# Moving eight vector adds into accumulating DMAs, and a residual update into a DRAM row scatter, in a fused state-space and expert kernel

## The chip, the cores and the metric

The kernel runs on one core of one Trainium2 chip. The metric is device time in microseconds (us) of one execution. Each profile shows one profiled execution; its span is about 2 us shorter than the timed figure of the same run. PE is the matmul engine (PEld its weight load), DVE the vector engine, ACT the scalar engine, POOL the engine that issues the accumulating DMAs, SP the engine that issues most others.

## The reference, cut to what matters

`x` has 2048 rows of 512 columns in bf16. `a` is a long convolution of `x` with a kernel built from 128 complex exponentials per column (done as a transform, spectral products, and an inverse transform) plus a skip term. `b` is `x`, with an expert's output added on the two rows with the largest router score.

```python
g = _sigmoid((x * gate_w).sum(-1, keepdims=True))
a = _A_ref(x, A_re, A_im, ...)          # y = irfft(rfft(x) * rfft(K)) + x * Dskip
# ... in _B_ref: the two rows with the largest r = x @ w_r
g_ = _silu(x_sel @ w_gate); u = x_sel @ w_up
y = (g_ * u) @ w_down                   # times sigmoid(r) of those rows
upd = _scatter_add(zero, flat_idx, y, axis=0)
b = x + upd
return g * a + (1 - g) * b
```

## The kernel before: the parts that matter

The program is a list of operations with their reads and writes. At build time a greedy scheduler orders the operations of each engine by its own cost model, and that order is then fixed. An engine that waits can't do work that comes later in that order, even if it is ready. Nearly all data lies in one on-chip tensor, so the profile names almost every tile `AR`. An operation is told by its source line (a helper's) and its form. Columns are done in two halves of 256 (`h` = 0, 1). The spectral products of each half come in two quarters (`qd`), each with a block 1, then a block 0.

The products of one quarter, all on DVE, with single buffers PA, PBb, PC and YY:

```python
for blk in blks:
    TT(v4(PA), xv(blk), kv(0, 0), MUL, ...)
    if blk == 1:
        TT(v4(PC), xv(0), kv(1, 0), MUL, ...)
        TT(PA, PA, PC, ADD, ...)                 # an add of 128x2048
    TT(v4(PBb), xv(blk), kv(0, 1), MUL, ...)
    if blk == 1:
        TT(v4(PC), xv(0), kv(1, 1), MUL, ...)
        TT(PBb, PBb, PC, ADD, ...)               # another: 8 in all
    TT(v1(YY, 0), v1(PA, 0), v1(PBb, 1), SUB, ...)
    TT(v1(YY, 1), v1(PA, 1), v1(PBb, 0), ADD, ...)
    TT(sd(0), y(0), y(1), ADD, ...); TT(sd(1), y(0), y(1), SUB, ...)
```

The inverse transform of one half (PE), its output gated and added to the residual `U`. For all but the last block, the adding was already a DMA before the change:

```python
# per block, q, t2, parity: 8 matmuls of 256 columns with the matrices G
if h == 0 or blk == 1:
    AC(YA(...), pb(...), ACTF.Copy, ..., scale=g)         # ACT
    g.dma_start(u, YA(...), accum_op=ADD)                  # POOL, 256 KB, rows of 512 B
else:
    STT(u, pb(...), g, u, MUL, ADD, ...)                   # DVE, the last block only
DMA(out, U ...)                                            # the stores
```

`U` was rewritten to `(1 - g) * (x + upd)` by `xupd`: two matmuls and one ACT copy for each of 16 row tiles. The order of the program:

```python
exps1(0); exps2(0)          # 41 exponentials on ACT; a half of exps2 parked in DRAM
routing(); tab1(0); forward(); tab2(0); tab1(1); xupd()
kgen(0); kp load; tab2(1); kspec(0); edges(0); kgen(1)
G load                      # c_inv, 2 MB: the inverse matrices
# kspec(1), products, inverse of both halves, stores
```

Of the kernel before, what the change touches and what calls it, by code (L numbers as in the profile page):

```python
# [9 lines left out]
BF = mybir.dt.bfloat16  # L10
# [44 lines left out]
class Op:  # L55
    __slots__ = ("eng", "fn", "deps", "cost", "tset", "prio", "idx", "pos", "start", "end", "sem", "n", "bl", "vc", "tag", "nbytes", "dma", "name", "alt")


class Prog:
# [4 lines left out]
    def __init__(self):  # L64
        self.bufs, self.ops, self.boost, self.bias = [], [], 0.0, {DVE: 0.4}

    def op(self, eng, fn, rd=(), wr=(), cost=0.2, tset=None, prio=0.0, tag="", n=1, nbytes=0, dma=False):
        o = Op()
        o.alt = None
        if isinstance(eng, tuple):  # L70
            o.alt = dict(zip(eng, zip(fn, cost)))
            eng, fn, cost = eng[0], fn[0], min(cost)
# [34 lines left out]
    def schedule(self):  # L107
# [25 lines left out]
        while left:  # L133
            best = None
            for e0 in ENGS:
                for o in ready[e0]:
                    if o.tset is not None and o.tset != phases[ph[0]]:
                        continue
                    e = e0
                    if o.alt is not None:  # L140
                        e = min(o.alt, key=lambda x: max(free[x], rt[o.idx]) + o.alt[x][1] + self.bias.get(x, 0.0))
                    st = max(free[e], rt[o.idx])
                    key = (st, -o.bl - o.prio)
                    if best is None or key < best[0]:
                        best = (key, o, e)
# [193 lines left out]
def bass_gated_mix__ssm_conv_s4__moe_arch_mod__prompt_kernel(nc, A_u, A_A_re, A_A_im, A_B_re, A_B_im, A_C_re, A_C_im, A_log_dt, A_Dskip,  # L339
# [5 lines left out]
    cb = np.concatenate([eye, np.zeros((128, 384), np.float32), sgn, -sgn], 1)  # L345
# [18 lines left out]
    with ExitStack() as es:  # L364
# [4 lines left out]
        dsem = [es.enter_context(nc.semaphore("d%d" % i)) for i in range(90)]  # L369
# [52 lines left out]

        o_ = [190 * KB]
# [4 lines left out]
        CB = small("cb", 1536, BF); CF = small("cf", 640, F32); AL = small("al", 2048, F32); B16 = small("b16", 2048, F32)  # L428
        WW = small("ww", 2048, BF); SG = small("sg", 256, F32); SGB = small("sgb", 128, BF); RTS = small("rts", 1088, F32)
        OHT = small("oht", 64, BF); ZB = small("zb", 2048, BF); WL = small("wl", 16, BF); XS = small("xs", 16, BF)  # L430
        HB = small("hb", 448, BF); MSB = small("msb", 16, BF); DSK = small("dsk", 1024, BF); OHR = small("ohr", 4096, BF)
# [18 lines left out]
        EB = [B("eb%d" % i, o, NM * 512) for i, o in enumerate((oG, oE))]  # L450
        ST = B("st", oE, NM * 512)
        PK = Buf(P, "park", AR[:, :], "dram", 0, 4, BF)
        park = nc.dram_tensor("park", (128, NM * 256), BF).ap()
# [7 lines left out]
        KC = [B("kc0", oD + 28 * KB, 3 * KB), B("kc1", oE + 11 * KB, 3 * KB)]  # L461
# [4 lines left out]
        PA = B("pa", oI, 4 * KB); PBb = B("pb", oI + 4 * KB, 4 * KB); PC = B("pc", oI + 8 * KB, 4 * KB); YY = B("yy", oI + 12 * KB, 4 * KB); YA = B("ya", oI + 16 * KB, 4 * KB)  # L466
# [30 lines left out]
        DQ([(CB(0, 128, 0, (1, 768)), cb_c[:, :])], [], [CB], 196608, eng=ACT)  # L497
# [14 lines left out]
        for buf, n in ((DSK, D), (OHR, L), (ZB, 2 * D)):  # L512
# [38 lines left out]
        def exps2(ts):  # L551
            for b in (EB[0], ST):
                P.op(POOL, lambda h, b=b: h.memset(b(0, 128, 0, (4 * NM, 64), (1, 4)), 1.0), [], [(b, ("e", 0))], cost=0.4)
            for i, m in enumerate(MAG2):
                if i:
                    AC(two(EB[0], ST, i * 4, 4 * NM), AL(0, 128, 0, (HC, 2), (4, 64), (1, 4)), ACTF.Exp, [AL], [(EB[0], ("e", i)), (ST, ("e", i))], scale=float(m), tset=ts)
# [70 lines left out]
        def routing():  # L627
# [14 lines left out]
            AC(SG(0, 128, 16, (1, 16)), SGB(0, 128, 0, (1, 16)), ACTF.Tanh, [(SGB, "s")], [(SG, "t")], scale=0.5, tset=1)  # L642
            TS(SGB(0, 128, 32, (1, 16)), SG(0, 128, 16, (1, 16)), 0.5, MUL, [(SG, "t")], [(SGB, "g")], s2=0.5, op1=ADD)
            CP(SG(0, 128, 32, (1, 16)), SGB(0, 128, 32, (1, 16)), [(SGB, "g")], [(SG, "g")])
            TS(SGB(0, 128, 48, (1, 16)), SGB(0, 128, 32, (1, 16)), -1.0, MUL, [(SGB, "g")], [(SGB, "o")], s2=1.0, op1=ADD)
            CP(SG(0, 128, 48, (1, 16)), SGB(0, 128, 48, (1, 16)), [(SGB, "o")], [(SG, "o")])
# [22 lines left out]
            AC(R(39), MSB(0, 128, 0, (1, 1)), ACTF.Tanh, [(MSB, 0)], [K("th")], scale=0.5, tset=1)  # L669
# [11 lines left out]
            for hf in range(2):  # L681
                bb = misc(True)
                def tro(h, bb=bb, hf=hf):
                    last = None
                    for t_ in range(8):
                        last = h.transpose(bb(0, 2, t_ * 128, (1, 128)), OHT(0, 128, (hf * 8 + t_) * 2, (1, 2)), IDN(0, (1, 128)))
                    return last
                P.op(PE, tro, [OHT, CB], [bb.buf], cost=0.5)
                EV(OHR(0, 2, hf * 1024, (1, 1024)), bb(0, 2, 0, (1, 1024)), [bb.buf], [(OHR, hf)])
# [14 lines left out]
            AC(hb(2), hb(0), ACTF.Silu, [(HB, 0)], [(HB, 2)], tset=1)  # L704
# [8 lines left out]
            CP(ZB(0, 2, 0, (1, D)), yb(0, 2, 0, (1, D)), [yb.buf], [(ZB, 0)])  # L713
            TS(ZB(0, 2, D, (1, D)), ZB(0, 2, 0, (1, D)), RTS(0, 2, 37, (1, 1)), MUL, [(ZB, 0), K("rs")], [(ZB, 1)])

# [111 lines left out]
        def products(h, qd, blks):  # L827
# [13 lines left out]
            for blk in blks:  # L841
                TT(v4(PA), xv(blk), kv(0, 0), MUL, kx(blk) + kk(0, 0), [PA])
                if blk == 1:
                    TT(v4(PC), xv(0), kv(1, 0), MUL, kx(0) + kk(1, 0), [PC])
                    TT(PA(0, 128, 0, (1, 2048)), PA(0, 128, 0, (1, 2048)), PC(0, 128, 0, (1, 2048)), ADD, [PA, PC], [PA])
                TT(v4(PBb), xv(blk), kv(0, 1), MUL, kx(blk) + kk(0, 1), [PBb])
                if blk == 1:
                    TT(v4(PC), xv(0), kv(1, 1), MUL, kx(0) + kk(1, 1), [PC])
                    TT(PBb(0, 128, 0, (1, 2048)), PBb(0, 128, 0, (1, 2048)), PC(0, 128, 0, (1, 2048)), ADD, [PBb, PC], [PBb])
                TT(v1(YY, 0), v1(PA, 0), v1(PBb, 1), SUB, [PA, PBb], [(YY, 0)])  # L850
                TT(v1(YY, 1), v1(PA, 1), v1(PBb, 0), ADD, [PA, PBb], [(YY, 1)])
                y = lambda pm: YY(0, 128, pm * 512, (1024, 2), (1, 512))
                sd = lambda pm: X(0, 128, h * 8192 + blk * 4096 + pm * 1024 + 2 * qd * 256, (2048, 2), (1, 512))
                kw = lambda pm: [xk(h, blk, part, pm, ft) for part in range(2) for ft in (2 * qd, 2 * qd + 1)]
                TT(sd(0), y(0), y(1), ADD, [YY], kw(0))
                TT(sd(1), y(0), y(1), SUB, [YY], kw(1))
# [3 lines left out]
        def inverse(h):  # L860
            for blk in (1, 0):
                bufs = {}
                for q in range(2):
                    for t2 in range(2):
                        for par in range(2):
# [4 lines left out]
                            def iv(hh, blk=blk, par=par, t2=t2, pb=pb, q=q):  # L870
                                last = None
                                for e in range(2):
                                    for c in range(4):
                                        part, ft = c % 2, 2 * q + c // 2
                                        last = hh.matmul(pb(0, 128, e * 256, (1, 256)), G(0, 128, ((par * 2 + part) * 4 + ft) * 512 + (2 * t2 + e) * 128, (1, 128)),  # L875
                                                         X(0, 128, h * 8192 + blk * 4096 + part * 2048 + (par * 4 + ft) * 256, (1, 256)), start=(q + e + c == 0), stop=(q == 1 and e == 1 and c == 3 and not t2))
# [3 lines left out]
                            P.op(PE, iv, [G] + [xk(h, blk, part, par, ft) for part in range(2) for ft in (2 * q, 2 * q + 1)] + ([KP, CO[h]] if q and t2 else []), [pb.buf], cost=8 * 0.11)  # L880
                            if q == 0:
                                continue
                            if h == 0 or blk == 1:
# [3 lines left out]
                                if par == 1:  # L887
                                    tbs = [blk * 8 + 4 * t2 + k for k in range(4)]
                                    u = U(0, 128, (blk * 8 + 4 * t2) * D + h * HC, (D, 4), (1, HC))
                                    P.op(POOL, lambda g, u=u, t2=t2: g.dma_start(u, YA(0, 128, t2 * 1024, (HC, 4), (1, HC)), accum_op=ADD), [(YA, (p_, t2, e)) for p_ in range(2) for e in range(2)] + [(U, ("x", tb)) for tb in tbs], [(U, ("o", tb, h)) for tb in tbs], cost=1.0, nbytes=262144, dma=True)  # L890
# [9 lines left out]
        def xupd():  # L900
            for tb in range(16):
                pb = fwp[(tb // 2) % 2]
                c0 = (tb % 2) * 512
                def xu(h, tb=tb, pb=pb, c0=c0):
                    h.matmul(pb(0, 128, c0, (1, D)), IDN(0, (1, 128)), U(0, 128, tb * D, (1, D)), start=True, stop=False)  # L905
# [88 lines left out]
```

## Time and profile before

| | before |
|---|---|
| time, median of 4 runs | 188.99 us (187.95 to 191.09) |
| span of the profiled run | 187.5 us |
| DVE busy | 157.1 us |
| first kernel-generation matmul of the second half (PE) | 123.1 us |
| last product on DVE ends | 179.2 us |
| from there to the end | 8.3 us |

The timeline of DVE before, from 120 us on (start, duration, engine, line, operation, count, and in brackets the idle time in front of it):

```profile
119.46 18.89 DVE L399 TENSOR_TENSOR AR<-AR 128x2048 bf16<-128x2048 bf16 x20
139.04 0.42 DVE L399 TENSOR_TENSOR AR<-ps,AR 8x256 bf16<-8x256 f32 x1 [0.69 <-PE ps L823]
139.49 39.68 DVE L399 TENSOR_TENSOR AR<-AR 128x2048 bf16<-128x2048 bf16 x46
180.55 3.71 DVE L406 SCALAR_TENSOR_TENSOR AR<-ps,AR 128x256 bf16<-128x256 f32 x8 [1.38 <-PE ps L875]
```

For sixty microseconds DVE idles 0.7 us, then does the last eight combines as the last inverse matmuls deliver.

### The profile page before, as it was taken

How to read it: one execution, taken by the hardware profiler on the slowest of the kernel's cores; microseconds unless marked ns; L12 is line 12 of the kernel's file. 1: busy time of each engine (PE TensorE's matmuls, PEld its weight loads, DVE VectorE, ACT ScalarE, POOL GpSimd, SP SyncE). 2: the span in 40 equal slices, each digit the busy share in tenths (PEclk: the TensorE clock that was granted, in tenths of full speed). 3: DMA queues.
4: the chain of work that ended last, by engine and by line, in shares of the span. 5: the costliest groups of instructions: out<-in, count | busy, mean ns of one | idle time of the engine just before them, and what ended most of it. 6: DMA issues, size and time to landing. Idle time of an engine off the chain costs nothing.

```text
span 187.5 us, 3219 instructions
## 1 busy us (share of the span) xinstructions
PE 139.4 (74%) x1318; PEld 90.7 (48%) x1318; DVE 157.1 (84%) x232; ACT 126.5 (67%) x210; POOL 12.3 (7%) x17
## 2 busy tenths in 40 slices
PE   0000599675999999999994997379879999375791
PEld 0000236232673444466561366278568888254680
DVE  0629124999999699999689999999989999999962
ACT  3699998999999763389999967637455573402400
POOL 8000000000000000000100000000000050500500
PEclk9999999999996999999999999958999999999998
DMA  5999999994039202200097000000840039591295
GB/s 98 309 300 357 278 258 264 405 378 108 3 91 355 61 0 56 56 3 0 19 416 310 0 3 0 2 0 3 273 180 0 0 40 151 77 154 33 33 146 157
DMA packets 33504, 25.20 MB, mean 134 GB/s; under 512 B 21449, under 2 KB 30802, under 8 KB 33106
## 3 DMA queue, kind: packets, MB, share of 16 engines
q1 hardware_dynamic: 28978, 23.10, 39.9%
q0 software_dynamic: 3168, 1.57, 7.7%
q10 hardware_dynamic: 1344, 0.33, 1.2%
q8 instruction: 10, 0.16, 0.4%
q14 instruction: 4, 0.03, 0.1%
HBM read 17.79 MB, written 2.75 MB: 110 GB/s over the span
## 4 chain that ended last, share of the span: by engine, by line
PE 45%; DVE 32%; ACT 7%; SPq 6%; DMA 4%; issue 3%; DVEq 0%
DVE AR L399 30%; PE ps L732 15%; PE ps L777 6%; PE ps L747 6%; SPq L495 6%; DMA AR<-c_fwd 4%; PE ps L875 4%; PE ps L791 3%; ACT AR L410 3%; ACT AR L414 2%; ACT AR L418 2%; PE ps L750 2%; PE ps L710 2%; PE ps L699 1%; PE ps L813 1%
## 5 line engine op out<-in xcount | busy, mean ns | idle before, releaser
L399 DVE TENSOR_TENSOR AR<-AR 128x1024 bf16<-128x1024 bf16 (+7 forms) x142 | 127.6, 949 | 11.2 <-DMA AR<-in_A_A_re_dram 6.0
L414 ACT ACTIVATE AR<-ps 128x1024 bf16<-128x1024 f32 (+4 forms) x55 | 42.2, 796 | 26.3 <-PE ps L813 11.8
L410 ACT ACTIVATE AR<-AR 128x512 bf16<-128x512 f32 (+5 forms) x73 | 50.4, 755 | 5.6 <-DVE AR L399 2.6
L732 PE MATMUL ps<-AR 128*128 128x512 bf16 x128 | 33.2, 413 | 24.4 <-DMA AR<-c_fwd 20.7
L875 PE MATMUL ps<-AR 128*128 128x256 bf16 x256 | 29.6, 273 | 7.8 <-DVE AR L399 7.8
L732 PEld LDWEIGHTS ps<-AR 128*128 128x128 bf16 x128 | 13.1, 106 | 42.1 <-DMA AR<-c_fwd 20.7
L875 PEld LDWEIGHTS ps<-AR 128*128 128x128 bf16 x256 | 24.7, 98 | 11.6 <-DVE AR L399 8.7
L410 ACT ACTIVATE AR<-ps,AR 128x256 bf16<-128x256 f32 (+1 forms) x40 | 19.8, 575 | 14.4 <-PE ps L875 13.5
L813 PE MATMUL ps<-AR 128*128 128x256 bf16 x160 | 19.2, 273 | 4.7 <-ACT AR L414 4.4
L813 PEld LDWEIGHTS ps<-AR 128*128 128x128 bf16 x160 | 15.0, 98 | 8.6 <-ACT AR L414 6.3
L414 DVE CAST AR<-ps 128x1024 bf16<-128x1024 f32 x6 | 7.3, 1218 | 13.1 <-PE ps L732 9.8
L747 PE MATMUL ps<-AR 128*128 128x512 bf16 x64 | 16.2, 389 | 0.0
L418 ACT ACTIVATE AR<-AR 128x256 int32<-128x256 f32 (+1 forms) x40 | 16.2, 468 | 0.1
L777 PE MATMUL ps<-AR 128*128 128x84 bf16 x256 | 13.7, 221 | 2.8 <-DVE AR L399 2.4
L777 PEld LDWEIGHTS ps<-AR 128*128 128x128 bf16 x256 | 12.7, 110 | 5.2 <-DVE AR L399 2.7
L890 POOL DMA_DIRECT2D AR<-AR x6 | 7.9, 1490 | 76.7 <-ACT AR L410 76.7
L403 DVE TENSOR_SCALAR AR<-AR 128x1024 int32<-128x1024 int32 (+5 forms) x22 | 11.4, 527 | 0.0
L747 PEld LDWEIGHTS ps<-AR 128*128 128x128 bf16 x64 | 5.8, 98 | 5.9 <-issue 0.2
L905 PE MATMUL ps<-AR 128*128 128x512 bf16 x16 | 6.2, 385 | 2.5 <-ACT AR L410 2.5
L791 PE MATMUL ps<-AR 128*32 128x128 bf16 (+1 forms) x96 | 6.4, 383 | 0.7 <-ACT AR L414 0.7
L931 POOL MEMSET AR<- 128x256 bf16 x2 | 0.6, 312 | 88.2 <-PE ps L777 88.2
L906 PE MATMUL ps<-AR 128*128 128x512 bf16 x16 | 6.1, 379 | 0.0
(48 smaller groups left out, 71.2 us busy)
## 6 DMA issues: line engine op xcount, KB each, us to landing
AR<-c_ksp SPq DMA_DIRECT2D x1, 2752.0 KB, 10.2
AR<-in_A_u_dram SPq DMA_DIRECT2D x2, 1024.0 KB, 7.7
AR<-c_fwd SPq DMA_DIRECT2D x1, 2048.0 KB, 8.1
AR<-c_fwdn SPq DMA_DIRECT2D x8, 256.0 KB, 3.8
AR<-c_inv SPq DMA_DIRECT2D x1, 2048.0 KB, 7.6
out_dram<-AR SPq DMA_DIRECT2D x16, 128.0 KB, 2.2
AR<-in_B_w_gate_dram SPq DMA_DIRECT2D x1, 1792.0 KB, 9.9
AR<-in_B_w_up_dram SPq DMA_DIRECT2D x2, 896.0 KB, 10.9
```

Of the source, the lines that this page charges most:

```text
L399: return P.op(DVE, lambda h: h.tensor_tensor(out=o, in0=a, in1=b, op=op), rd, wr, cost=tt_cost(o, a, b), **k)
L403: return P.op(DVE, lambda h: h.tensor_scalar(out=o, in0=a, scalar1=s1, scalar2=None, op0=op0), rd, wr, cost=c, **k)
L410: return P.op(ACT, lambda h: h.activation(out=o, in_=a, func=func, scale=scale, bias=bias), rd, wr, cost=0.185 + nel(o) * 0.833e-3 + (0.09 ...
L414: return P.op((ACT, DVE), (lambda h: h.activation(out=o, in_=a, func=ACTF.Copy), lambda h: h.tensor_copy(o, a)), rd, wr, cost=(0.185 + n * ...
L418: return P.op((ACT, DVE), (lambda h: h.activation(out=o, in_=a, func=ACTF.Copy, scale=c), lambda h: h.tensor_scalar(out=o, in0=a, scalar1= ...
L495: P.op(SP, lambda h: h.dma_start_transpose(PRM(0, 128, i * D, (1, D)), dr(prm[i], 0, (128, D), (1, 128))), [], [(PRM, i)], cost=1.25, nbyt ...
L732: last = h.matmul(o, F(0, 128, ((par * 4 + st) * 2 + part) * 512 + ft * 128, (1, 128)), U(0, 128, (blk * 8 + st * 2 + par) * D, (1, D)), s ...
L747: last = h.matmul(o, ng(0, 128, (st * 2 + part) * 128, (1, 128)), U(0, 128, (blk * 8 + st * 2 + 1) * D, (1, D)), start=False, stop=(st == ...
L777: last = hh.matmul(pb(0, 128, (g - b0) * 84, (1, 84)), TP[h][1 - part](0, 128, g * 128, (1, 128)), TQ[h][1 - part](0, 128, g * 84, (1, 84) ...
L791: last = hh.matmul(pb(32 * g, 32, c4, (256, njg), (4, 64)), lw, KA[h](0, 128, c4 + 4 * (base[0] + g), (16, njg), (84, 64)), start=True, st ...
L813: last = hh.matmul(pb(0, 128, n * 256, (1, 256)), KP(0, 128, u * 2048 + tau * 128, (1, 128)), KC[h](0, 128, jg * 256, (1, 256)), start=(k ...
L875: last = hh.matmul(pb(0, 128, e * 256, (1, 256)), G(0, 128, ((par * 2 + part) * 4 + ft) * 512 + (2 * t2 + e) * 128, (1, 128)), X(0, 128, h ...
```

## The change

The intent: take eight of the 142 vector operations away (the 128x2048 adds) and let DMA do them; take 32 matmuls and 16 ACT copies of the residual rewrite away; take nine exponentials from ACT's first phase.

- The eight adds become accumulating DMAs of 512 KB, issued by POOL. The products get double buffers, and the differences are formed in place.
- The two expert rows are scatter-added to a DRAM copy of the input. That copy is loaded into `U` in place of the input.
- The output becomes `g * (a - b) + b`: 32 added matmuls with a negative identity subtract `b` in the inverse.
- `exps2` moves behind the first sines, without its trip to DRAM.

The diff, cut to its core:

```diff
+        def accum(o, i, rd, wr, nbytes):
+            P.op(POOL, lambda h: h.dma_start(o, i, accum_op=ALU.add), rd, wr, cost=1.4, nbytes=nbytes, dma=True)
...
             for blk in blks:
+                PA, PBb = PAB[qd]
                 TT(v4(PA), xv(blk), kv(0, 0), MUL, kx(blk) + kk(0, 0), [PA])
-                if blk == 1:
-                    TT(v4(PC), xv(0), kv(1, 0), MUL, kx(0) + kk(1, 0), [PC])
-                    TT(PA(...), PA(...), PC(...), ADD, [PA, PC], [PA])
                 TT(v4(PBb), xv(blk), kv(0, 1), MUL, kx(blk) + kk(0, 1), [PBb])
                 if blk == 1:
-                    TT(v4(PC), xv(0), kv(1, 1), MUL, kx(0) + kk(1, 1), [PC])
-                    TT(PBb(...), PBb(...), PC(...), ADD, [PBb, PC], [PBb])
-                TT(v1(YY, 0), v1(PA, 0), v1(PBb, 1), SUB, [PA, PBb], [(YY, 0)])
-                TT(v1(YY, 1), v1(PA, 1), v1(PBb, 0), ADD, [PA, PBb], [(YY, 1)])
+                    for part in range(2):
+                        p, q = (PA, PBb)[part], PCD[h][qd][part]
+                        TT(v4(q), xv(0), kv(1, part), MUL, kx(0) + kk(1, part), [q])
+                        accum(p(0, 128, 0, (1, 2048)), q(0, 128, 0, (1, 2048)), [q], [p], 524288)
+                TT(v1(PA, 0), v1(PA, 0), v1(PBb, 1), SUB, [PBb], [PA])
+                TT(v1(PA, 1), v1(PA, 1), v1(PBb, 0), ADD, [PBb], [PA])
...
+                                    if q:      # in the inverse: minus identity times U
+                                        last = hh.matmul(pb(0, 128, e * 256, (1, HC)), CB(0, 128, 768, (1, 128)), U(...), start=False, ...)
...
-        def xupd(): ...                       # 32 matmuls, 16 ACT copies
-        exps2(0)
-        DMA(park <- ST); ... DMA(EB[1] <- park)
+        exps2(2)
+        DMA([(xp[:, :], dr(A_u, ...))], [], [XP], 2097152, prio=1e5)
...
+            indirect_dma_start(xp[:, :], rows IDX, ZB(0, 2, 0, (1, D)), compute_op=ADD)
+        DMA(U <- xp)                          # 2 MB, after the scatter
-        tab2(0, (1, 1)); tab1(1, (1, 1)); tab2(1, (1, 1))
+        tab2(0, (3, 3)); tab1(1, (3, 3)); tab2(1, (3, 3))   # later phase; tanh, silu too
```

## The prediction

> **What bounds the kernel now.** The page gives DVE 157.1 us busy of 187.5, PE 139.4, ACT 126.5. The table by stretches shows DVE full from about 33 us to 179 us (61 of 64 us up to 97, nearly all after that); the chain of waits is PE and ACT from 33 to 97 us, but alternates with a DVE that is full as well. From 97.6 us it is DVE: second-half table work to 122.3 us, then spectral products to 179.2 us (about 56 us of TENSOR_TENSOR, 2048 columns at 1.15 us spacing, 1024 at about 0.6), then 8.3 us of tail: last inverse matmuls, eight combines of 0.48 us, the store. Before 33 us DVE is half idle; ACT runs 41 exponentials until 28.4 us, 0.52 us apart.
>
> **What the change moves.**
> 1. Eight DVE adds of 128x2048 leave the products: 8 x 1.15 = 9.2 us of a full DVE. Eight accumulating DMAs of 512 KB replace them. The six accumulating DMAs of 256 KB in the trace take 1.3 to 1.75 us to issue and land after 4.2 to 5.4 us; their 512-byte packets take 74 ns against 27 ns for plain stores of that size. Now rows are 4 KB: between 0.28 us (overhead-bound guess) and 0.59 us (linear) a packet, estimated 2.3 to 4.7 us per transfer, one after the other. [...] At the middle, 3.4 us, each half's four accumulations take about 14 us plus 5 us of issue and landing, longer than the multiplications that could hide them, so DVE waits 2 to 4 us per half. Net gain in the products: about 3.5 us (0 if linear, 7 if overhead-bound).
> 2. The residual rewrite goes: 32 PE matmuls (0.22 us each, 7 us), 16 ACT copies (9.8 us), 16 small transposes, one 1.0 us ACT and one 0.67 us DVE copy. They lie beside a full DVE: mostly off the path, about 1 us of gain.
> 3. Subtraction by 32 added PE matmuls of 256 columns: 32 x 0.11 = 3.5 us, of which about 0.9 us in the tail.
> 4. Nine exponentials (4.7 us) move behind the first sines. DVE can start near 28 us instead of 33. But ACT is full until 56 us, and pays two more table loads (1.28 us each), so the second table comes hardly earlier. Gain 1 to 2 us.
> 5. DRAM copy (2 MB), row scatter and 2 MB reload replace the 640 KB park round trip. All are early, off the path; the copy sits ahead of the up-weights, which land near 48 us instead of 42 and are needed at 54.
>
> **Sum.** Minus 2.5 us before 97 us, minus 3.5 us in the products, plus 0.9 us of matmuls and about 0.5 us because the late block's accumulations hold the end: minus 4.6 us. Predicted 184.0 us, range 178.5 to 188.5. Chances: faster 0.60, same 0.31, slower 0.09.
>
> **What the profile would show.** Right: DVE busy near 146 us; DVE waits on the accumulating DMAs of 2 to 4 us in each products stage; 4 KB packets near 0.43 us; ACT with four table loads; 32 more matmuls at the inverse; table stage of the second half starting near 95 us. The first sine would start near 25 us.
>
> **What would make it wrong.** Accumulations at the linear cost, or slowed by the 2 MB inverse-matrix load falling into the first products: no gain at all. Overhead-bound packets: 180 us. The weights or forward matrices held behind the DRAM copy: PE stalls near 50 us. A static order that puts an accumulation behind one that waits.

The 0.59 us is eight times the 74 ns measured for a packet of 512 bytes. The 0.28 us is the author's guess; adding the 47 ns by which that packet is dearer than a plain store to eight times 27 ns would give 0.26 us, an estimate.

## More of the kernel before

From the page of the kernel before: busy time; the rows of the span in 40 slices (tenths; PEclk is the clock that PE was granted); the chain of waits by engine and by line; the costliest group; the load of the inverse matrices.

```profile
PE 139.4 (74%) x1318; PEld 90.7 (48%) x1318; DVE 157.1 (84%) x232; ACT 126.5 (67%) x210; POOL 12.3 (7%) x17
...
DVE  0629124999999699999689999999989999999962
...
PEclk9999999999996999999999999958999999999998
DMA  5999999994039202200097000000840039591295
...
PE 45%; DVE 32%; ACT 7%; SPq 6%; DMA 4%; issue 3%; DVEq 0%
...
L399 DVE TENSOR_TENSOR AR<-AR 128x1024 bf16<-128x1024 bf16 (+7 forms) x142 | 127.6, 949 | 11.2 <-DMA AR<-in_A_A_re_dram 6.0
...
AR<-c_inv SPq DMA_DIRECT2D x1, 2048.0 KB, 7.6
```

DVE is full in nearly every slice from the eighth to the third from the end. The chain gives PE more than DVE, because until about 97 us both are full. From there to the end DVE leads.

## The result, and the profile after

The time rose from a median of 188.99 us to one of 200.97 us (199.51 to 201.10, 4 runs). The ratio is 1.064, with a 95% interval of 1.056 to 1.071. Ratios here are the mean time of one kernel's fast runs over that of the other's fast runs of the same rounds, so they are not quite the ratio of the medians quoted beside them.

| milestone | before | after | added up to here |
|---|---|---|---|
| first kernel-generation matmul, second half | 123.1 | 125.4 | +2.3 |
| last product on DVE ends | 179.2 | 186.7 | +7.5 |
| end of the profiled run | 187.5 | 199.3 | +11.8 |

So in these two profiles 2.3 us are lost before 125 us, 5.2 us in the products, though eight adds went from there, and 4.3 us in the tail (12.6 us in place of 8.3). The first of these is not firm. Nine runs below (e1, e5 to e9, e11, e13 and e16) have the DVE order of the changed kernel up to its first accumulation, and their profiles put the first milestone anywhere from 122.3 to 126.0 us.

The page of the kernel after, with the lines that answer to those of before, and the group of the accumulations:

```profile
PE 141.0 (71%) x1302; PEld 93.4 (47%) x1302; DVE 150.7 (76%) x229; ACT 116.5 (58%) x190; POOL 31.6 (16%) x25
...
DVE  0628129999599999987999999959339997839442
...
PEclk9999999995887999999985998599999999697999
DMA  5999999988039202200599100299920079997195
...
PE 36%; DVE 30%; DMA 23%; SPq 6%; issue 2%; POOL 0%; DVEq 0%
DVE AR L400 24%; DMA AR<-AR 14%; PE ps L731 13%; PE ps L874 6%; SPq L501 6%; PE ps L746 6%; DMA AR<-c_ksp 5%; DMA AR<-c_fwd 4%; PE ps L776 2%; DVE AR L415 2%; PE ps L812 2%; DVE AR L404 2%; PE ps L705 2%; PE ps L749 2%; PE ps L694 1%
...
L400 DVE TENSOR_TENSOR AR<-AR 128x2048 bf16<-128x2048 bf16 (+6 forms) x135 | 118.6, 928 | 25.3 <-DMA AR<-AR 13.6
...
L713 POOL DMA_INDIRECT xp<-AR x1 | 14.5, 14522 | 70.7 <-DVE AR L404 70.7
...
AR<-AR POOLq DMA_DIRECT2D x8, 512.0 KB, 7.7
...
AR<-c_inv SPq DMA_DIRECT2D x1, 2048.0 KB, 11.6
```

DVE did get lighter, by 6.4 us. But its tensor operations now idle 25.3 us in place of 11.2. Over half of that, 13.6 us, is ended by a DMA from `AR` to `AR`, the accumulations. In the chain DMA went from 4% to 23%. The accumulations are 14 of these; 5 are the load of `c_ksp`, where PE waited, but DVE had table work in all that time and did not idle for it. One more line has changed that the change didn't touch: the same 2 MB load of `c_inv` takes 11.6 us in place of 7.6.

The timeline of DVE after, from 120 us on, in the columns of before:

```profile
119.39 11.64 DVE L400 TENSOR_TENSOR AR<-AR 128x2048 bf16<-128x2048 bf16 x13
131.46 1.23 DVE L400 TENSOR_TENSOR AR<-AR 128x2048 bf16<-128x2048 bf16 x1 [0.43 <-DMA AR<-AR]
134.51 6.15 DVE L400 TENSOR_TENSOR AR<-AR 128x2048 bf16<-128x2048 bf16 x7 [1.82 <-DMA AR<-AR]
141.26 0.42 DVE L400 TENSOR_TENSOR AR<-ps,AR 8x256 bf16<-8x256 f32 x1 [0.60 <-PE ps L822]
147.62 18.66 DVE L400 TENSOR_TENSOR AR<-AR 128x1024 bf16<-128x1024 bf16 x22 [5.94 <-DMA AR<-AR]
167.65 5.74 DVE L400 TENSOR_TENSOR AR<-AR 128x1024 bf16<-128x1024 bf16 x7 [1.37 <-DMA AR<-AR]
177.48 9.23 DVE L400 TENSOR_TENSOR AR<-AR 128x1024 bf16<-128x1024 bf16 x13 [4.08 <-DMA AR<-AR]
191.68 0.88 DVE L407 SCALAR_TENSOR_TENSOR AR<-ps,AR 128x256 bf16<-128x256 f32 x2 [4.97 <-PE ps L877]
```

The solid block of before is cut at five places, each time by an accumulation: 8.2 us of waits in the first half, 5.45 us in the second. The prediction had 2 to 4 us for each. Why does an accumulation take so long? Here are the records of the eight in the trace, with what else was on the DMA queues:

| issued, us | landed after, us | what was under way beside it |
|---|---|---|
| 126.8 | 4.6 | nothing |
| 129.1 | 5.4 | the one before, for 2 us |
| 133.0 | 12.1 | the `c_inv` load, issued at 133.65 |
| 136.0 | 11.6 | the same, and the one before |
| 159.7 | 4.7 | nothing at first |
| 160.8 | 6.8 | the one before, then two output accumulations |
| 165.4 | 8.6 | two output accumulations of 256 KB, issued at 161.4 and 162.1 and so ahead of it, and stores |
| 166.6 | 10.9 | the same, and the one before |

The packets themselves were cheap. The records that belong to these DMAs have 4096 bytes each, 1024 of them for eight transfers, with a median of 339 ns, less than the 0.43 us that the prediction assumed. (In the same trace the packets of 512 bytes took a median of 74 ns in the output accumulations and 27 ns in the plain stores.) From 136 to 142 us the records of the 16 DMA engines show about 16 accumulation packets of 4 KB and 16 load packets of 16 KB in each microsecond, one for one: 95 of the one kind and 96 of the other in all. Below, "turns" stands for this sharing as counted here; that each engine alternates strictly between the two was not shown. So each of the 16 engines gets through one accumulation packet in a microsecond there, on average, in place of about three at 131 or at 144 us (49 and 52 packets in that microsecond), when no load is beside it.

In the second half the records show another kind of sharing. There POOL's transfers come in the order of issue. From 167 to 170 us their queue shows only the 512-byte packets of the two output accumulations, 808 of them. The third product accumulation had been issued at 165.4 us, but its packets come after them, from 170 us on.

The tail can be read from the chain of waits after, cut to its end (start, duration, what):

```profile
136.03 11.56 DMA AR<-AR
147.62 17.54 DVE AR L400 x21
...
166.58 10.88 DMA AR<-AR
177.48 3.11 DVE AR L400 x5
180.63 0.61 PE ps L874 x4
...
182.31 0.85 PE ps L874 x4
...
187.06 3.93 PE ps L874 x36
191.10 0.44 PE ps L874 x4
```

The accumulation that landed at 177.5 us was a block 1's. Once it had landed PE still had half of block 1's inverse and all of block 0's to do, and the chain stays on PE from 180.6 us to 195.1 us. From 181.3 to 184.7 us PE ran at half clock: four matmuls took 0.85 us at 182.3 us, 0.44 us at 191.1 us. (The expectations call such a stretch a cold clock.) In this trace the granted clock is at one half in stretches of 3.4 and 6.8 us, two of 3.4 us in the last inverse (from 171.1 and 181.3 us), just after idle times of PE of 4.5 and 4.4 us. In the last inverse of the kernel before, idle times of 3.25 and 3.53 us were followed by no half clock. The second stretch, of 3.4 us at half rate, cost about 1.7 us of the chain, an estimate (half its length).

The front shows the third loss. ACT loads its tables at 24.16, 42.81 and 49.83 us, besides the first, which was there before; the first sine starts at 25.45 us, as predicted. The earlier sines gave DVE table work early, and the routing's small operations fell behind it. The timeline of PE before, in the same columns as DVE's:

```profile
45.90 0.27 PE L655 MATMUL ps<-AR 128*128 128x128 f32 x1
46.01 1.89 PE L732 MATMUL ps<-AR 128*128 128x512 bf16 x8
47.82 1.76 PE L677 MATMUL ps<-AR 128*128 128x2 bf16 x64
```

The timeline of PE after:

```profile
46.30 0.48 PE L659 MATMUL ps<-AR 128*128 128x128 f32 x1 [3.09 <-DVE AR L404]
47.44 3.60 PE L731 MATMUL ps<-AR 128*128 128x512 bf16 x8 [0.66 <-DVE AR L415]
50.83 0.42 PE L659 MATMUL ps<-AR 128*128 128x128 f32 x1
51.04 2.19 PE L731 MATMUL ps<-AR 128*128 128x512 bf16 x8
53.06 1.75 PE L681 MATMUL ps<-AR 128*128 128x2 bf16 x64
```

The gather of the routed rows (64 matmuls of 2 columns) starts at 53.06 us, 5.2 us later than before. This profile is an extreme one: the other runs with late exponentials start it at 50.2 to 52.7 us, those with early ones at 47.8 to 49.5 us. Eight forward matmuls took 3.60 us in place of 1.89, at half clock (granted 0.5 from 44.8 to 51.6 us). The second half's tables, predicted to start near 95 us, started at 101.18 us; before it was 97.57 us.

### The profile page after: what moved, and what is told of

It is laid out like the page before. It is cut to its first block, busy times and chain, and to the rows that moved or that the text cites. A ratio compares the mean times of both kernels' runs of the same rounds, so it can differ in the third digit from the quotient of the medians.

```text
span 199.3 us, 3178 instructions
## 1 busy us (share of the span) xinstructions
PE 141.0 (71%) x1302; PEld 93.4 (47%) x1302; DVE 150.7 (76%) x229; ACT 116.5 (58%) x190; POOL 31.6 (16%) x25
## 4 chain that ended last, share of the span: by engine, by line
PE 36%; DVE 30%; DMA 23%; SPq 6%; issue 2%; POOL 0%; DVEq 0%
DVE AR L400 24%; DMA AR<-AR 14%; PE ps L731 13%; PE ps L874 6%; SPq L501 6%; PE ps L746 6%; DMA AR<-c_ksp 5%; DMA AR<-c_fwd 4%; PE ps L776 2%; DVE AR L415 2%; PE ps L812 2%; DVE AR L404 2%; PE ps L705 2%; PE ps L749 2%; PE ps L694 1%
## 5 line engine op out<-in xcount | busy, mean ns | idle before, releaser
L400 DVE TENSOR_TENSOR AR<-AR 128x2048 bf16<-128x2048 bf16 (+6 forms) x135 | 118.6, 928 | 25.3 <-DMA AR<-AR 13.6
L415 ACT ACTIVATE AR<-ps 128x1024 bf16<-128x1024 f32 (+3 forms) x51 | 39.4, 806 | 36.4 <-PE ps L812 16.6
L731 PE MATMUL ps<-AR 128*128 128x512 bf16 x128 | 34.6, 425 | 22.5 <-DMA AR<-c_fwd 21.9
L874 PE MATMUL ps<-AR 128*128 128x256 bf16 x256 | 35.5, 286 | 10.8 <-DVE AR L400 8.9
L731 PEld LDWEIGHTS ps<-AR 128*128 128x128 bf16 x128 | 13.3, 107 | 40.6 <-DMA AR<-c_fwd 21.9
L425 POOL DMA_DIRECT2D AR<-AR x14 | 14.7, 1178 | 78.0 <-DVE AR L400 61.0
L812 PE MATMUL ps<-AR 128*128 128x256 bf16 x160 | 20.5, 286 | 8.4 <-DMA AR<-c_ksp 5.4
L713 POOL DMA_INDIRECT xp<-AR x1 | 14.5, 14522 | 70.7 <-DVE AR L404 70.7
L411 ACT ACTIVATE AR<-ps,AR 128x256 bf16<-128x256 f32 x24 | 9.8, 472 | 23.7 <-DMA AR<-AR 11.8
L812 PEld LDWEIGHTS ps<-AR 128*128 128x128 bf16 x160 | 15.9, 103 | 12.6 <-DMA AR<-c_ksp 5.7
L776 PE MATMUL ps<-AR 128*128 128x84 bf16 x256 | 13.9, 220 | 6.1 <-DVE AR L400 5.9
L415 DVE CAST AR<-ps 128x1024 bf16<-128x1024 f32 (+2 forms) x9 | 9.7, 1080 | 9.8 <-PE ps L731 8.7
L746 PE MATMUL ps<-AR 128*128 128x512 bf16 x64 | 17.1, 411 | 0.0
L776 PEld LDWEIGHTS ps<-AR 128*128 128x128 bf16 x256 | 12.6, 110 | 8.6 <-DVE AR L400 6.2
L877 PE MATMUL ps<-AR 128*128 128x256 bf16 x32 | 9.2, 286 | 0.0
L407 DVE SCALAR_TENSOR_TENSOR AR<-ps,AR 128x256 bf16<-128x256 f32 x8 | 3.5, 480 | 5.8 <-PE ps L877 5.2
L419 DVE TENSOR_SCALAR AR<-AR 128x256 int32<-128x256 f32 (+1 forms) x24 | 6.5, 307 | 0.5 <-ACT AR L411 0.4
## 6 DMA issues: line engine op xcount, KB each, us to landing
AR<-c_inv SPq DMA_DIRECT2D x1, 2048.0 KB, 11.6
```

What stands on the lines that cost most here:

```text
L400: return P.op(DVE, lambda h: h.tensor_tensor(out=o, in0=a, in1=b, op=op), rd, wr, cost=tt_cost(o, a, b), **k)
L411: return P.op(ACT, lambda h: h.activation(out=o, in_=a, func=func, scale=scale, bias=bias), rd, wr, cost=0.185 + nel(o) * 0.833e-3 + (0.09 ...
L415: return P.op((ACT, DVE), (lambda h: h.activation(out=o, in_=a, func=ACTF.Copy), lambda h: h.tensor_copy(o, a)), rd, wr, cost=(0.185 + n * ...
L419: return P.op((ACT, DVE), (lambda h: h.activation(out=o, in_=a, func=ACTF.Copy, scale=c), lambda h: h.tensor_scalar(out=o, in0=a, scalar1= ...
L425: P.op(POOL, lambda h: h.dma_start(o, i, accum_op=ALU.add), rd, wr, cost=1.4, nbytes=nbytes, dma=True)
L713: P.op(POOL, lambda h: h.indirect_dma_start(xp[:, :], bass.IndirectOffsetOnAxis(ap=IDX(0, 2, 0, (1, 1)).bitcast(mybir.dt.uint32), axis=0), ...
```

## The experiments

The theory after this reading: the accumulations lose because they share the DMA queues, in the first half with the load of the inverse matrices, in the second with the output's own accumulations, and because DVE's fixed order can't step over the wait; the late exponentials lose about 3 us besides. The rivals: the residual rewrite or the added matmuls cost the time; a clock effect; the accumulations themselves are slow; the new buffers or order.

All kernels were timed beside the kernel before on the same chip in the same session. Medians are of all runs; ratios use fast runs. Two are an exception: of e11 and e12 two of the four runs each are listed as slow, and the ratios in the table don't leave them all out. From the runs listed as fast alone they would be about 1.005 (e11) and 1.013 (e12).

| run | median, us | ratio to before [95%] | DVE waits for accumulations, us |
|---|---|---|---|
| (after) | 200.97 | 1.064 [1.056, 1.071] | 13.6 |
| e1 | 192.02 | 1.014 [1.005, 1.023] | 0 |
| e2 | 197.88 | 1.042 [1.036, 1.049] | 12.6 |
| e3 | 198.80 | 1.048 [1.040, 1.055] | 14.3 |
| e4 | 192.34 | 1.013 [1.007, 1.020] | 0 |
| e5 | 196.65 | 1.037 [1.022, 1.052] | 8.0 |
| e6 | 195.30 | 1.032 [1.019, 1.045] | 5.2 |
| e7 | 199.96 | 1.057 [1.043, 1.070] | 13.3 |
| e8 (wrong result) | 193.51 | 1.017 [1.003, 1.031] | 7.5 |
| e9 | 199.46 | 1.054 [1.046, 1.062] | 11.5 |
| e10 | 200.09 | 1.057 [1.050, 1.064] | 8.6 |
| e11 (wrong result) | 192.00 | 1.013 [1.002, 1.024] | 0 |
| e12 | 193.68 | 1.024 [1.016, 1.031] | 0 |
| e13 (wrong result) | 188.68 | 0.996 [0.989, 1.003] | 4.7 |
| e14 | 192.41 | 1.008 [1.001, 1.015] | 0 |
| e15 | 195.96 | 1.024 [1.014, 1.035] | 0.3 |
| e16 | 191.73 | 1.009 [1.003, 1.016] | 0 |
| e17 | 192.85 | 1.021 [1.013, 1.029] | 4.8 |
| e18 | 190.25 | 1.001 [0.992, 1.011] | 0.2 |

### Which part of the change loses the time (e1 to e4)

e1 is the kernel after with its eight accumulations turned back into vector adds:

```diff
-                        accum(p(0, 128, 0, (1, 2048)), q(0, 128, 0, (1, 2048)), [q], [p], 524288)
+                        TT(p(0, 128, 0, (1, 2048)), p(0, 128, 0, (1, 2048)), q(0, 128, 0, (1, 2048)), ADD, [q], [p])
```

> The changed kernel with its eight accumulating DMAs of 512 KB put back as eight DVE adds, nothing else undone. Theory A (the accumulations cost the most: DVE waits 13.6 us for them, and they push the last inverse late): about 192.5 us, DVE's wait for accumulations gone, products stage near 56 us, tail after the last product near 9 us. Rival B (the loss was made before the products, by the moved exponentials and the colder PE clock; the accumulations are about neutral): 200 us or more, since DVE gets 9.2 us more work.

It took 192.02 us. The accumulations alone cost about 9 us of the 12. DVE did 8 us more work (158.9 us busy) and was done with the products 9.2 us earlier (177.5 us). Of these 9.2 us, 2.9 lie before the first kernel-generation matmul of the second half, where DVE does the same in both: that is the scatter of single profiles. The stage from there to the last product took 55.0 us in place of 61.3. The tail after it is nearly as long as with the accumulations, 12.1 us against 12.6.

e2 is the kernel after with the exponentials in the first phase again:

```diff
-        exps2(2)
+        exps2(0)
-        tab2(0, (3, 3)); tab1(1, (3, 3)); tab2(1, (3, 3))   # and tanh, silu
+        tab2(0, (1, 1)); tab1(1, (1, 1)); tab2(1, (1, 1))
```

> The changed kernel with the nine exponentials back before the first sines (two table loads fewer). Theory A: a gain of 2 to 4 us only (the second half's table stage starts near 98 instead of 101 us), so about 198 us. Rival B: about 191 us.

It took 197.88 us, 3.1 us less than the kernel after (4.0 us by the two ratios).

e3 is the kernel before with nothing but the new products: double buffers, in-place differences, accumulations.

```diff
-   (the products of before)      +   (the products of after, PAB, PCD, accum)
```

> The kernel before with the products summed by DMA, nothing else of the change (no residual rewrite, exponentials where they were). Theory A: about 196 to 198 us, DVE waits over 10 us for accumulations. Rival B: 185 to 189 us.

It took 198.80 us, 9.1 us more than the kernel before, with 14.3 us of waits on DVE. Nothing else of the change is in it.

e4 is the kernel before with nothing but the late exponentials (e2's edit the other way round).

> The kernel before with only the nine exponentials moved behind the first sines. Theory A: 190 to 192 us (start of the second half's table stage 2 to 3 us later). Rival B: 195 us or more.

It took 192.34 us, 2.6 us more than the kernel before. So both losses were shown from both sides: about 9 us for the accumulations and 2.6 to 4 us for the late exponentials, together the whole 12 us within the noise. By this balance the rest of the change comes out near zero; e12 below, which runs the rest alone, doesn't fully bear that out.

### Why the accumulations lose (e5 to e9, e13)

e5 keeps the accumulations in the first half only, e6 in the second only:

```diff
-                        accum(...)
+                        (accum(...)) if h == 0 else TT(p, p, q, ADD, ...)      # e5; h == 1 in e6
```

> The changed kernel with accumulating DMAs in the products of the first half only; the second half's four sums are DVE adds. All DVE adds gave 192.0, all DMA 201.0. Theory A1 (the first half loses because its third and fourth accumulation share the DMA queues with the 2 MB load of the inverse matrices): DVE waits about 8 us there and saves 4.6, so about 195.5 us. Rival A2 (the loss is all in the second half, where accumulations, output accumulations and stores fill the DMA engines): 189 us, below all DVE adds.

> The changed kernel with accumulating DMAs in the products of the second half only. Theory A1 plus a loss of the second half (waits of 5.5 us, a longer PE tail after a cold start of its clock): about 197 us. If the loss were all in the first half: 188 us.

They took 196.65 and 195.30 us. Beside e1 (192.02 us), that is 4.6 us for the first half's and 3.3 us for the second half's. The intervals of these two ratios are about 1.5% each way, so only that both halves lose is firm, not the split. In e6 the load of the inverse matrices took 7.5 us again, in e5 11.4 us: the two slow each other.

e7 tried to make the load's packets smaller by describing its rows as eight pieces:

```diff
-        DMA([(G(0, 128, 0, (1, 8192)), g_c[:, :])], [], [G], 2097152)
+        DMA([(G(0, 128, 0, (1024, 8), (1, 1024)), <the same, rows in 8 pieces>)], [], [G], 2097152)
```

> The changed kernel, the 2 MB load of the inverse matrices cut into 2 KB pieces instead of 16 KB ones; same bytes, same order on every engine. If the accumulations of 4 KB packets wait their turn behind 16 KB packets (turns by packet), the third and fourth land after 6 to 8 us instead of 12, the load itself later than 11.6 us: the first half's wait falls from 8 to about 4 us, 197 to 199 us in all. If it is only bytes that count, nothing changes: 201 us.

It took 199.96 us, but tells nothing: the trace shows packets of 16 KB as before, not the smaller ones that were meant. It counts as one more run of the kernel after.

e8 loads only a sixteenth of the inverse matrices, so that the result is wrong:

```diff
+        DMA([(G(0, 128, 0, (1, 512)), <the first 512 columns of g_c>)], [], [G], 2097152)
```

> The changed kernel with one sixteenth of the inverse matrices loaded (wrong result on purpose; engine orders the same). If the load is what delays the first half's third and fourth accumulation, they land after 4.6 to 5.5 us as the first two do, DVE's wait of 5.9 us before 147.6 us goes, and the time is about 195 us; the second half's waits stay. If not, 200 us or more.

It took 193.51 us. The third and fourth accumulation landed after 5.8 and 5.3 us in place of 12.1 and 11.6, and the waits fell to 7.5 us. This says that the load is what stretched them.

e9 splits the load into four, each with rows of 4 KB, with the right result:

```diff
+        DMA([(G(0, 128, 2048 * i, (1, 2048)), g_c[:, 2048 * i:2048 * i + 2048]) for i in range(4)], [], [G], 2097152)
```

> The changed kernel with the 2 MB load of the inverse matrices issued as four loads of 4 KB rows (the 2 KB pieces before were joined to 16 KB packets again, so that run tested nothing). The trace shows one accumulation packet for one 16 KB packet in turn. If turns by packet are the cause, the third and fourth accumulation land after 7 to 8 us instead of 12 and 11.5, DVE's longest wait falls from 5.9 to under 2.5 us, total 197 us. If bytes decide, no change: 200 to 201 us.

The third accumulation now landed after 7.0 us, but the fourth after 10.4, and the last piece of the load only at 146.5 us. The waits fell by 2 us and the time by 1.5 us, hardly more than the scatter of the runs. In this run the four smaller loads dealt out the time otherwise but made no room: from the first accumulation's issue to the last landing of load and accumulations it took 20.8 us, as in the kernel after.

e13 clears both halves' queues: e8's cut, and the first half's output accumulations cut to 16 columns of a row. Its result is wrong too.

```diff
+    G load: 512 of 8192 columns
+    accum(U(..., (1, 16)) if h == 0 else u, YA(..., (1, 16)) if h == 0 else YA(...), ...)
```

> The changed kernel, all eight product accumulations by DMA, one sixteenth of the inverse matrices loaded and the first half's four output accumulations cut to 16 columns of one block (wrong result on purpose; DVE, PE and ACT orders the same). If sharing of the DMA queues makes the waits, all eight land in 4.5 to 7.5 us, DVE's waits for them fall from 13.6 to about 5 us, and the time is 189 to 191 us (with the load alone cut it was 193.5). If the waits come from issue and order, they stay near 7.5 us and the time near 193.5.

It took 188.68 us, a ratio of 0.996: the whole loss is gone, with all eight accumulations in place, with the late exponentials still there, and with the DVE order of the kernel after. All of them landed in 4.6 to 7.9 us. Beside e1 (ratio 1.014) they even gain 1.8%, some 3.4 us with an uncertainty of about 2, and the prediction had put 3.5 us on them. No run made the same cuts with vector adds, but in e1's trace no engine waits for that load or for an output accumulation, so e1 had little to gain from them. From the waits of e13:

```profile
DVE AR L400 <- DMA AR<-AR: 4.7, 3, 2.5
```

That is total, number of waits and longest, to be set against 13.6, 5 and 5.9 in the kernel after. A rival falls here, that the accumulations are slow in themselves.

### The rest of the change, and the order (e10 to e12, e14 to e16)

e10 put accumulations into the kernel before, in the first half only, with single buffers in the second half and the load split as in e9:

```diff
+                        (accum(...)) if h == 0 else TT(p, p, q, ADD, ...)
+                PA, PBb = PAB[qd * (1 - h)]              # single buffers in the second half
+        DMA([... for i in range(4)])                     # the load of G as in e9
```

> The kernel before with accumulating DMAs for the first half's four sums only, the second half's products in the old order with DVE adds, and the inverse matrices loaded as four loads of 4 KB rows: nothing else of the change. If the accumulations are worth something where the queues are free: 4.6 us of DVE work less, 2 to 3 us of waits, 186.5 to 188 us against 189.5. If even there they only return what they save: 189 to 191 us.

It took 200.09 us, a miss. DVE's waits were 8.6 us, and the scheduler also gave another order: the last inverse started at 176.4 us in place of 163.8 and the end came 16 us after the last product. Nor were the queues free: the third and fourth accumulation landed after 10.5 us beside the load. What of the loss comes from the order can't be told apart, so it is inconclusive.

e11 is e1 without the subtraction in the inverse (wrong):

```diff
-                                    if q:
-                                        last = hh.matmul(pb(...), CB(0, 128, 768, (1, 128)), U(...), ...)
```

> The changed kernel with DVE adds, and the 32 subtracting matmuls left out (wrong result on purpose). With them PE ran without a pause from the start of the last inverse to its end, 12.1 us of tail after the last product against 8.3 before. If the subtraction costs what its 16 matmuls in that stretch take (16 x 0.11 = 1.8 us): 190.2 us. If nothing: 192 us.

Its ratio is 1.013 beside 1.014 of e1, but that counts a slow run. Its two fast runs (190.50 and 190.60 us) are about 1.5 us below e1's median. In the profile PE ends 2.0 us earlier but the span is only 0.9 us shorter. So the 32 added matmuls cost about 1 to 1.5 us, not far from the 0.9 us predicted, with the noise as large as that.

e12 is the residual rewrite alone: e1's and e2's edits together.

> The changed kernel with DVE adds and the exponentials first: of the change, the residual rewrite (DRAM copy, row scatter, reload, subtraction in the inverse) and the new product buffers are left. The parts so far add up: 192.0 minus 2.5 to 3 us, so about 189 us, the same as before within 1%. If the parts interact, under 187 or over 191 us.

Its runs lie from 190.80 to 194.54 us, and the profiled one was the fastest, with a span of 189.0 us. From e1 and e2 one would expect about 189 us. The timed runs are longer than that. Why three came out at over 193 us was not settled. They go with a lower granted clock, 0.915 in the mean beside 0.944 of the fastest run. The runs of e14 and e15 pair in the same way (190.2 us at 0.945 beside 192.5 at 0.923; 193.1 at 0.938 beside 196.0 at 0.916).

e14 is e12 with single product buffers, to bring the old order of the products back:

```diff
-        PAB = [(SL[0], SL[2]), (SL[4], SL[5])]
-        PCD = [[(SL[1], SL[3])] * 2, [(SL[6], SL[7]), (SL[8], SL[9])]]
+        PAB = [(SL[0], SL[2])] * 2
+        PCD = [[(SL[1], SL[3])] * 2] * 2
```

> The changed kernel with DVE adds, exponentials first, and one pair of product buffers for both quarters as before: of the change only the residual rewrite and the in-place differences are left. If the second pair of buffers, by letting the scheduler mix the two quarters' products, is what starts the last inverse 2.5 us late on a cold clock: last inverse starts near 164 us instead of 166.9, tail back to about 9 to 9.5 us, 0.99 to 1.0 of before. If the subtraction makes the tail: 1.01 or more.

The tail came back to 8.4 us (12.1 us in e1, 11.0 in e12), but the last product ended at 182.4 us in place of e12's 178.0. The two profiles are not quite alike, since e14's is one at the lower clock (0.923 beside 0.944). Still, the best runs of both are level (190.2 and 190.8 us): the order trades one for the other, with no net gain.

e15 is e14 with one quarter's two accumulations, in the first half, and double buffers there:

```diff
+                        (accum(...)) if h == 0 and qd == 0 else TT(p, p, q, ADD, ...)
```

> As the one before, but the two sums of the first half's first quarter by accumulating DMA (two pairs of buffers in the first half only). They are issued before the load of the inverse matrices and should land in 4.6 and 5.4 us. If an accumulation with free queues pays: 2.3 us of DVE work less, waits under 1.5 us, 0.5 to 1 us better than the one before. If its latency can't be hidden in the static order: 1 us or more worse.

The two landed after 4.6 and 4.5 us and DVE waited 0.3 us. All the same it took 195.96 us: PE and DVE got another order, and the end came 15.3 us after the last product. Here the loss is not one of DMA at all, but of the order that the scheduler chose.

e16 is e1 with 40 matmuls without use in front of the last inverse. They fill a wait of PE, 4.8 us in e1, after which the granted clock was 0.5 for 6.8 us:

```diff
+     [hh.matmul(fwp[0](...), CB(0, 128, 0, (1, 128)), CB(0, 128, 512, (1, 256)), ...) for n_ in range(40)]
```

> The changed kernel with DVE adds (192.0 us, 1.014 of before) and 40 matmuls of 256 columns into an unused PSUM bank in PE's idle time of 4.8 us before the last inverse; all other orders the same. There the granted clock was 0.5 for 6.8 us and the first 36 matmuls took 6.4 us instead of 4.1. If the cold clock is a term of the tail: no half clock in the last inverse, PE ends about 2.3 us earlier, 189.7 us, ratio 1.002. If not: 192 us or more.

The half clock was gone from the last inverse: its 36 matmuls took 4.1 us in place of 6.4. The ratio of 1.009 beside 1.014 of e1 is about 1 us, within the noise of about 2. So in e1 the half clock went with that wait of PE, and about 1 us is the best estimate of its cost in e1; the 2.3 us of the theory aren't excluded.

### Moving the load out of the way (e17, e18)

e17 is the kernel after with one added wait, and a right result. The load of the inverse matrices waits for the first half's four accumulations, through a token that they write and it reads:

```diff
+        TOK = Buf(P, "tok", AR[:, :], "token", 0, 4, BF)
-                        accum(..., [q], [p], 524288)
+                        accum(..., [q], [p] + ([(TOK, (qd, part))] if h == 0 else []), 524288)
-        DMA([(G(0, 128, 0, (1, 8192)), g_c[:, :])], [], [G], 2097152)
+        DMA([(G(0, 128, 0, (1, 8192)), g_c[:, :])], [TOK], [G], 2097152)
```

> The kernel after with one wait added: the 2 MB load of the inverse matrices starts only when the first half's four accumulations have landed. Correct result. If turns taken with that load are what make the third and fourth accumulation of the first half take 12 us, all four now land in 4 to 8 us, the waits of the first half's differences fall from about 8 to about 2 us, and the time falls from 201 to about 195 us (the second half's waits stay near 5.5). If the cost is in the accumulations themselves, or the load then comes too late for the first inverse, the time stays at 199 to 202 us.

It took 192.85 us, 8 us less than the kernel after and better than expected. The first half's four accumulations landed after 6.3, 4.6, 5.0 and 5.0 us. The load started at 139.7 us in place of 133.6 and took 7.6 us again. From the waits and the page of e17:

```profile
DVE AR L400 <- DMA AR<-AR: 4.8, 3, 3.2
...
AR<-AR POOLq DMA_DIRECT2D x8, 512.0 KB, 5.5
...
AR<-c_inv SPq DMA_DIRECT2D x1, 2048.0 KB, 7.6
```

The load came 2 us later (147.4 us against 145.3), and PE had other matmuls until then. The token also shifted the order: the first accumulation was issued at 113.4 us in place of 126.8. That shift is not what gained. e2 happens to have it too (113.1, 125.8, 128.1 and 131.9 us), with the load at 131.1 us, and its fourth accumulation landed after 11.4 us. Its waits, 7.5 us of them in the first half, where e17 has 1.0:

```profile
DVE AR L400 <- DMA AR<-AR: 12.6, 4, 6.0
```

What is left in e17 is in the second half, from its timeline of DVE:

```profile
160.37 7.80 DVE L400 TENSOR_TENSOR AR<-AR 128x1024 bf16<-128x1024 bf16 x10 [0.63 <-DMA AR<-AR]
171.34 7.79 DVE L400 TENSOR_TENSOR AR<-AR 128x1024 bf16<-128x1024 bf16 x10 [3.17 <-DMA AR<-AR]
```

There the last accumulation still took 9.4 us, behind one of the output's. So e18 takes e17, makes the second half's adds vector adds again, and puts the exponentials first (e2's edit):

> e17 with two more edits: the phase-0 exponentials before the first sines again, and accumulation in the first half only, vector-engine adds in the second. Correct result. If the three causes found so far (late exponentials 2.5 to 3 us, first-half queue sharing 6 us, second-half waits 5.5 us) add up, 186 to 190 us, that is level with the kernel before or a little faster. If the fixed instruction order or the later last inverse takes the gain back, as in e10 and e15, 192 to 197 us.

It took 190.25 us (187.90 to 191.57, 6 runs), a ratio of 1.001 [0.992, 1.011]: level with the kernel before, and in the range expected. Its four accumulations landed after 4.6, 5.1, 4.5 and 5.5 us, and DVE waited 0.2 us in all. The last product ended at 175.7 us, 3.4 us before the 179.2 us of the kernel before, though the span is only 0.6 us shorter. Where those 3 us went is shown by the busy times from 148 to 183 us, first of the kernel before, then of e18. The columns are the stretch, its length, PE, PEld, DVE, ACT and POOL busy (with counts), granted clock, DMA share and GB/s.

```profile
148.00:183.00 35.00, 27.18 (x247) 23.57 (x245) 33.20 (x43) 12.46 (x27) 7.91 (x6) 1.00 0.55 86
```

```profile
148.00:183.00 35.00, 34.80 (x319) 30.95 (x317) 30.20 (x40) 13.86 (x28) 7.69 (x6) 1.00 0.56 88
```

In the kernel before, DVE fills this stretch and PE has 8 us free. In e18 PE is full, 34.8 of 35 us. The inverse matmuls by source line, first before, then e18 (shortest, median and longest in ns, then first and last start in us), show when it began:

```profile
L875 PE MATMUL ps<-AR x256: 272/273/283, 141.7 to 183.0; 128*128 128x256 bf16 x128
```

```profile
L874 PE MATMUL ps<-AR x256: 272/273/273, 147.7 to 182.3; 128*128 128x256 bf16 x128
```

In e18 the inverse starts 6 us later. Its matrices landed at 144.9 us in place of 138.9, and the fixed order of PE has more of the second half's kernel spectrum in front of it. From then on PE has no gap to the end. So what DVE gained runs into a full PE. How much of the 6 us the later load made is open. The second half's kernel generation had also started 3.8 us later than before (126.9 us in place of 123.1), and PE shows no wait for the load itself. That the later load moved PE's order is argued from the traces; no run had the one without the other.

## Why the prediction was wrong, point by point

**The step that failed** is the first, "DVE waits 2 to 4 us per half. Net gain in the products: about 3.5 us". Measured were waits of 8.2 and 5.45 us, and a net loss of about 9 us (e1, e3). The packet price was no part of the miss: 0.34 us against the 0.43 us assumed. What was wrong is the overlap. The prediction summed each half's four transfers without any other traffic, to 14 plus 5 us, and took all but 2 to 4 us of that to be hidden behind DVE's own work. The records give, from a half's first issue to its last landing:

| | after, first half | after, second half | e13, first half | e13, second half |
|---|---|---|---|---|
| four accumulations, us | 20.8 | 17.8 | 14.6 | 13.9 |
| DVE's waits for them, us | 8.2 | 5.45 | 2.3 | 2.5 |
| difference: what DVE's work hid, us | 12.6 | 12.3 | 12.3 | 11.4 |

So about 12 us can be hidden, not the 15 to 17 that the prediction implies. With free queues the four take about 14 us and the waits stay small. With the queues shared they take 4 to 6 us more, and nothing hides that. The lengthening sits in two accumulations of each half: 12.1 and 11.6 us to landing beside the load of the inverse matrices, 8.6 and 10.9 us behind the output's own accumulations. That the prediction's 19 us a half lie close to the 20.8 and 17.8 measured is luck, since it had no other traffic in them. That its gain of 3.5 us reappears in e13 as about 3.4 us is partly luck too: there its transfers were too long and its hiding too large, and the two errors cancel. It did name the load as a danger ("slowed by the 2 MB inverse-matrix load falling into the first products: no gain at all") but gave it no price. The trace of before had both times needed: the load was issued at 131.3 us, and the products ran from about 122 us on. The result was not "no gain" but 9 us lost. In the profiles the waits of 13.6 us, less the 8.2 us of DVE work saved (beside e1), make 5.4 us of it. The rest is not resolved: the profiles of e1 and of the kernel after differ by 2.9 us before the first accumulation, and their tails by 0.5 us only. The second collision, with the output's accumulations, was not named at all.

**The tail.** Predicted was 0.9 us for the added matmuls and 0.5 us for the late block. The matmuls cost about 1 to 1.5 us (e11). The tail grew by 4.3 us. In the kernel after it starts from the accumulation that landed at 177.5 us. With vector adds in the new buffers it is still 12.1 us (e1), so most of its growth needs no accumulation. It goes with the order of the products in the second pair of buffers, which e14 undid at the price of later products. How it divides between that order and the added matmuls was not settled.

**The exponentials.** Predicted was "DVE can start near 28 us instead of 33" and a gain of 1 to 2 us; measured was a loss of 2.6 us (e4) to 3.1 us (e2; 4.0 by the ratios). The first sine did come at 25.45 us and the four table loads came as named. The step that failed is that an earlier start on DVE was counted as an earlier end. What DVE did earlier was table work; the routing's operations came later, and PE waited for them (3.09 us at 46.3 us in the profile after) and ran at half clock there (from 44.8 to 51.6 us). That the loss comes from the late exponentials is shown; that it runs over these waits of PE is read from the traces and was not tested by itself.

**The residual rewrite and the scatter.** Predicted was about 1 us of gain, off the path. In the balance of e1 to e4 it is near zero. The direct run, e12, shows no gain: its ratio is 1.024 (1.013 from its fast runs), and its best run, 190.80 us, is 0.9 us above the median of the kernel before timed beside it. So rewrite and new buffers together cost up to about 5 us, and why stays open. The scatter and the reload were off the path, as predicted: no engine waits for them in the profile after. The scatter of two rows of 1 KB held POOL for 14.5 us there and landed 15.6 us after its issue; in e2, e12, e14, e15 and e18, with early exponentials, it held POOL for 21.9 us (28.1 us to landing in e18).

**DVE busy** near 146 us was predicted, 150.7 measured. **The second table stage** near 95 us was predicted, 101.18 measured.

## What to carry to other kernels

To replace an operation on a full engine by a DMA, price the DMA from issue to landing, in the very microseconds in which it will run, with every other transfer of that stretch on the same queues. The cost of a packet on an idle queue says little: here the same 512 KB took 4.6 us alone, 12.1 us beside a 2 MB load, and 8.6 us behind two smaller transfers on its own queue. Then count how much work there is to hide it, here 12 us a half. Where the two meet, first look whether the large load can wait; here one added dependence gave 8 of the 12 us back. And if the program's order is fixed at build time, a wait stops everything behind it and each small edit may move the order, so time the parts both alone and taken away.
